# Linear attention block: x tile 1 transposed by the DMA crossbar instead of TensorE, and the Wk blocks dealt out anew over two DMA queues

## The chip, the cores and the metric

One core of one Trainium2 chip runs the kernel. The metric is device time in microseconds (us) of the whole program. The kernel before takes 99.58 us, the median of 3 runs (99.29 to 100.04).

## The reference: what is computed

```python
B, S, D = 1, 2048, 640;  H = 32; Dh = 20
qkv = (x @ wqkv)                       # split into q, k, v of 32 heads
phi = lambda t: where(t > 0, t + 1, exp(t)) + 1e-6
pq, pk = phi(q), phi(k)
kv  = einsum("bhsd,bhse->bhde", pk, v)
z   = einsum("bhsd->bhd", pk)
o   = einsum("bhqd,bhde->bhqe", pq, kv) / (einsum("bhqd,bhd->bhq", pq, z) + 1e-6)
return o @ wo
```

All inputs and the output are bfloat16. x is 2048 x 640, wqkv is 640 x 1920, wo is 640 x 640.

## The kernel before, in words

The 2048 rows of x are 16 tiles of 128 rows (st = 0 to 15); the 640 columns are 5 blocks of 128 (c = 0 to 4). Three of the buffers matter here. `xT` holds x transposed, which every projection needs as TensorE's stationary or moving operand. `xn` holds x as it lies in memory, which the later product of pk with x needs. `wk` holds the K columns of wqkv as five row blocks, called Wk blocks 0 to 4 (160 KB each).

The program is recorded by hand. `P.add(engine, ...)` appends an instruction to one engine's list and works out from the named tiles which semaphores it waits for. So the order on each engine is the order of the `P.add` calls. DMAs are instructions of the queue that issues them, SyncE ("sp") or ScalarE ("act").

TensorE's own order is: warm-up matmuls on constants (L283), the transposes of the first tiles (L200), the K projection of all 16 tiles (`k_half`, L293: two halves of 320 columns, five matmuls each, one for every block c), and after that the products of pk and x (L317), the Q projection (L354), the small products (L445, L472, L544) and the output projection (L576).

How the first stage is put together:

- `XCH` (L181) cuts the rows into seven pieces: tile 0, tile 1, tile 2, tiles 3 and 4, tiles 5 to 7, tiles 8 to 11, tiles 12 to 15. The first `NPE` = 2 pieces (L180) come through TensorE. The others come by `load_xT` (L187), one `dma_start_transpose` each on SyncE, straight from memory into `xT`.
- `load_wk` (L235) sets the order of the first DMAs. SyncE issues the left half of x tile 0, then Wk blocks 0, 2 and 3. ScalarE issues the right half of x tile 0, then x tile 1 ("x12"), then Wk blocks 1 and 4. In those strings "w23" is the block from 2 to 3.
- `load_xT` follows on SyncE with the five transposing DMAs, and `load_rest` (L258) with the Q weights, x tiles 2 to 15 for `xn` in three DMAs, the V weights and wo.
- `transpose_x(st, part)` (L193) transposes two or three 128 x 128 blocks of a tile on TensorE into PSUM; VectorE (part 0, L212) or ScalarE (part 1, L209) copies the result to `xT`.
- The string at L630 is TensorE's order for tiles 0 and 1: "k00a" is block 0 of tile 0, half a (one matmul), "t1a" is the first part of tile 1's transpose, "k10" is block 0 of tile 1, both halves (two matmuls). From tile 2 on each tile's ten matmuls stand together (L640).
- `k_phi` (L302) turns a tile's K into pk: an exponential on ScalarE, then two instructions on VectorE.

Of the kernel before, what the change touches and what calls it, by code (L numbers as in the profile page):

```python
# [84 lines left out]
def bass_standalone__linear_attn_block__prompt_kernel(nc, x, wqkv, wo, out):  # L85
# [15 lines left out]
    with contextlib.ExitStack() as ctx:  # L101
# [75 lines left out]
                    band(bm[:, GT * t:GT * (t + 1)], [[-DH if lo else DH, 3], [0, DH]],  # L177
                         -64 * t if lo else DH - 1 + 64 * t, 1 if lo else -1, "bm")

        NPE = 2  # L180
        XCH = [(0, 128), (128, 256),  # L181
               (256, 384), (384, 640), (640, 1024), (1024, 1536), (1536, 2048)]

        def xch_of(row):
            return next(i for i, (a, b) in enumerate(XCH) if a <= row < b)

        def load_xT():  # L187
            for i, (a, b) in enumerate(XCH[NPE:]):
                P.add("sp", lambda e, a=a, b=b: e.dma_start_transpose(
                    xT[:, :].rearrange("p (c s) -> p c s", s=S)[:, :, a:b], x[0, a:b, :]),  # L190
                    writes=[("xT", NPE + i)], dma=True)

# [22 lines left out]
        def xT_keys(a, b, cs=range(NC_)):  # L215
            keys = []
            for i, (p, q) in enumerate(XCH):
                if p < b and a < q:
                    keys += [("xT", i)] if i >= NPE else sorted(
                        {("xT", i, 0 if c < 2 else 2) for c in cs})  # L220
            return keys

        def w_cols(dst, lo, hi, col, key, eng):
            P.add(eng, lambda e: e.dma_start(
                dst[:, 0:NC_ * D].rearrange("p (c n) -> p c n", n=D)[:, :, lo:hi],
                wqkv[:, col + lo:col + hi].rearrange("(c p) n -> p c n", p=128)),
                writes=[key], dma=True)

        def load_xn(a, b, eng):
            P.add(eng, lambda e: e.dma_start(  # L230
                xn[:, a * D:b * D].rearrange("p (t n) -> p t n", n=D),
                x[0, 128 * a:128 * b, :].rearrange("(t p) n -> p t n", p=128)),
                writes=[("xn", t) for t in range(a, b)], dma=True)

        def load_wk():  # L235
            tl = mybir.InstLoadActFuncSet(
                name=nc.get_next_instruction_name(),
                act_func_set_id=ACT_TABLE_SET_LN_EXP, ins=[], outs=[])
            P.add("act", lambda e: e.add_instruction(tl), writes=["table"])
            for eng, lo in (("sp", 0), ("act", HALF)):  # L240
                P.add(eng, lambda e, lo=lo: e.dma_start(
                    xn[:, lo:lo + HALF], x[0, 0:128, lo:lo + HALF]),
                    writes=[("xn", 0, lo)], dma=True)
            for eng, what in (("sp", "w01 w23 w34"), ("act", "x12 w12 w45")):
                for k in what.split():
                    a, b = int(k[1]), int(k[2])
                    if k[0] == "x":
                        load_xn(a, b, eng)
                    else:
                        P.add(eng, lambda e, a=a, b=b: e.dma_start(  # L250
                            wk[:, a * D:b * D].rearrange("p (c n) -> p c n", n=D),
                            wqkv[128 * a:128 * b, D:2 * D].rearrange("(c p) n -> p c n", p=128)),
                            writes=[("wk", c) for c in range(a, b)], dma=True)
# [3 lines left out]

        def load_rest():  # L258
            w_cols(wqn, 0, D, 0, "wqn", "sp")
            for a, b in ((2, 8), (8, 12), (12, 16)):  # L260
                load_xn(a, b, "sp")
            for g, n in ((0, 5), (5, 1)):
                f = min(GT, gsz[g])
                k = gsz[g] // f * n
                for d in range(NC_):
                    P.add("sp", lambda e, g=g, f=f, k=k, d=d: e.dma_start(
                        wv[:, 128 * NG * d:128 * NG * (d + 1)].rearrange(
                            "p (j f) -> p j f", f=64)[:, 2 * g:2 * g + k, 0:f],
                        wqkv[128 * d:128 * (d + 1), 2 * D + goff[g]:2 * D + goff[g] + k * f].rearrange(
                            "p (j f) -> p j f", f=f)),  # L270
                        writes=[("wv", i, d) for i in range(g, g + n)], dma=True)
            for t in range(2):
                P.add("sp", lambda e, t=t: e.dma_start(
                    wog[64 * t:64 * t + GT, 0:5 * D].rearrange("p (g n) -> p g n", n=D),
                    wo[0:5 * GW, :].rearrange("(g t p) n -> t p g n", t=2, p=GT)[t]),
                    writes=[("wog", g, t) for g in range(5)], dma=True)
            P.add("sp", lambda e: e.dma_start(
                wog[0:gsz[5], 5 * D:6 * D], wo[goff[5]:, :]),
                writes=[("wog", 5, 0)], dma=True)

        def warm(n, cols=BK):
            for _ in range(n):
                P.add("pe", lambda e: e.matmul(  # L283
                    bank(4, cols), nc.const_aps.tensor(1.0, [128, 128], BF16),
                    nc.const_aps.tensor(1.0, [128, cols], BF16), start=True, stop=True),
                    writes=[("bank", 4)])
# [333 lines left out]

        pool_const()
        load_wk()
        load_xT()
        load_rest()
        warm(5)
        warm(1, 128)
        for part in range(2):
            transpose_x(0, part)
        warm(1)
        order = "k00a t1a k00b t1b k10 k01 k11 k02 k12 k03 k13 k04 k14"  # L630
        for k in order.split():
            st, part = int(k[1]), "ab".find(k[-1])
            if k[0] == "t":
# [127 lines left out]
```

## Time and profile before

| what | value |
|---|---|
| median of 3 runs | 99.58 us (99.29 to 100.04) |
| the profiled execution's own time | 99.56 us |
| its span in the profile | 98.3 us |
| TensorE matmuls (PE) busy | 95.1 us, 97% of the span |
| VectorE / ScalarE / GpSimd busy | 63.7 / 48.8 / 4.7 us |
| K projection, L293 | 160 matmuls, 22.8 us |
| DMA moved | 12.60 MB, mean 128 GB/s |

The span is what the profile covers, from the first to the last instruction; 1.26 us of the execution's time lie around it. In the profile PE is TensorE's matmul side and PEld its weight loads, DVE is VectorE, ACT is ScalarE, POOL is GpSimd, SP is SyncE. SPq and ACTq rows are DMA issues: their length is the time that the queue's sequencer spent on the issue, not the transfer. The landing of a transfer is given apart, counted from the start of its issue. A matmul's shown duration contains its pipeline, so the step from one start to the next is the rate. All times in microseconds are from the span's start, if nothing else is said.

### The profile page before, as it was taken

To read this page: it belongs to the slowest core of one execution; us is meant where nothing else is said; L and a number is where in the kernel's file an instruction comes from. 1 tells how busy PE (TensorE), PEld (TensorE's weight loads), DVE (VectorE), ACT (ScalarE), POOL (GpSimd) and SP (SyncE) were. 2 spreads that over 40 slices of the span, in tenths; PEclk is the share of its full clock that TensorE was granted. 3 is DMA by queue.
4 is the path that set the end of the run, shared out by engine and by line. 5 is a ranking of instruction groups with operands and counts; after the bars stand their busy time and mean duration, and the time that the engine had idled before them with its cause. 6 is when DMAs were issued, how large, how long until landed. Compare 5 with 4: busy or idle time off the path is not lost.

```text
span 98.3 us, 1814 instructions
## 1 busy us (share of the span) xinstructions
PE 95.1 (97%) x694; PEld 61.2 (62%) x699; DVE 63.7 (65%) x124; ACT 48.8 (50%) x93; POOL 4.7 (5%) x19
## 2 busy tenths in 40 slices
PE   6999999999999999999999999999999999999991
PEld 2467777777755444445687867655557677777771
DVE  5314998888899439997839836758999206272222
ACT  5116455544526120005806456796988765453532
POOL 6500000000000000000000520000000000000000
DMA  2999999999998294000340023313200335532334
GB/s 48 320 269 194 238 157 111 350 366 360 316 169 108 21 239 80 0 0 0 63 77 7 0 63 93 94 32 86 79 0 0 133 74 168 205 117 87 130 133 137
DMA packets 26369, 12.60 MB, mean 128 GB/s; under 512 B 18553, under 2 KB 26361, under 8 KB 26361
## 3 DMA queue, kind: packets, MB, share of 16 engines
q1 hardware_dynamic: 25640, 11.87, 50.2%
q10 hardware_dynamic: 720, 0.61, 1.9%
q8 instruction: 5, 0.08, 0.3%
q14 instruction: 4, 0.02, 0.1%
HBM read 5.90 MB, written 2.62 MB: 87 GB/s over the span
## 4 chain that ended last, share of the span: by engine, by line
PE 95%; ACT 2%; issue 0%
PE ps L293 23%; PE ps L576 22%; PE ps L354 22%; PE ps L317 21%; PE ps L283 3%; ACT w2g L483 2%; PE ps L445 1%; PE ps L544 1%; PE ps L200 1%; PE ps L472 1%; ACT osb L599 0%
## 5 line engine op out<-in xcount | busy, mean ns | idle before, releaser
L317 PE MATMUL ps<-pk,xn 128*128 128x480 bf16 (+1 forms) x160 | 23.2, 299 | 0.0
L293 PE MATMUL ps<-wk,xT 128*128 128x320 bf16 x160 | 22.8, 303 | 0.0
L354 PE MATMUL ps<-xT,wqn 128*128 128x512 bf16 x95 | 22.0, 379 | 0.4 <-issue 0.2
L576 PE MATMUL ps<-w2p,pq 128*128 128x320 bf16 (+2 forms) x170 | 22.1, 291 | 0.0
L293 PEld LDWEIGHTS ps<-wk,xT 128*128 128x128 bf16 x160 | 15.6, 98 | 6.8 <-DMA wk<-in_wqkv_dram 0.9
L576 PEld LDWEIGHTS ps<-w2p,pq 128*128 128x128 bf16 x170 | 15.9, 98 | 6.2 <-issue 0.2
L317 PEld LDWEIGHTS ps<-pk,xn 128*128 128x128 bf16 x160 | 13.6, 98 | 9.4 <-issue 0.3
L362 ACT ACTIVATE eq<-ps 128x512 bf16<-128x512 f32 x20 | 11.9, 597 | 13.8 <-PE ps L354 13.6
L354 PEld LDWEIGHTS ps<-xT,wqn 128*128 128x128 bf16 x100 | 11.5, 118 | 9.1 <-issue 0.3
L306 ACT ACTIVATE ek<-ps 128x640 bf16<-128x640 f32 x16 | 11.2, 704 | 10.7 <-PE ps L293 10.1
L599 ACT CAST osb<-ps 128x320 bf16<-128x320 f32 (+2 forms) x27 | 11.0, 413 | 9.7 <-PE ps L576 9.0
L311 DVE SCALAR_TENSOR_TENSOR pk<-ps,ek 128x640 bf16<-128x640 f32 x16 | 13.2, 825 | 0.5
L569 DVE TENSOR_TENSOR pq<-pq,rd 128x512 bf16<-128x512 bf16 x20 | 7.3, 418 | 4.2 <-DMA rd<-rdc 4.2
L375 DVE TENSOR_SCALAR eq<-eq 128x512 bf16<-128x512 bf16 x20 | 5.8, 288 | 5.9 <-ACT eq L362 5.8
L602 DVE CAST osb<-ps 128x320 bf16<-128x320 f32 (+1 forms) x7 | 3.2, 456 | 8.7 <-PE ps L576 8.7
L308 DVE TENSOR_SCALAR ek<-ek 128x640 bf16<-128x640 bf16 x16 | 5.2, 325 | 5.3 <-ACT ek L306 5.1
L366 ACT ACTIVATE rq<-ps 128x512 bf16<-128x512 f32 x13 | 7.7, 592 | 0.0
L339 ACT CAST pt<-ps 128x480 bf16<-128x480 f32 x4 | 2.2, 562 | 8.2 <-PE ps L317 8.1
L379 DVE TENSOR_TENSOR pq<-eq,rq 128x512 bf16<-128x512 bf16 x13 | 5.5, 426 | 1.1 <-ACT rq L366 0.7
L388 DVE TENSOR_TENSOR za<-pk 128x1280 f32<-128x1280 bf16 x4 | 5.8, 1482 | 0.0
L382 DVE SCALAR_TENSOR_TENSOR pq<-ps,eq 128x512 bf16<-128x512 f32 x7 | 4.8, 692 | 0.2
L388 DVE TENSOR_TENSOR za<-za 128x1280 f32<-128x1280 f32 x3 | 4.4, 1486 | 0.0
(37 smaller groups left out, 36.7 us busy)
## 6 DMA issues: line engine op xcount, KB each, us to landing
out_dram<-osb SPq DMA_DIRECT2D x15, 160.0 KB, 1.8
xn<-in_x_dram SPq DMA_DIRECT2D x2, 640.0 KB, 8.9
xn<-in_x_dram SPq DMA_DIRECT2D x1, 960.0 KB, 7.0
wqn<-in_wqkv_dram SPq DMA_DIRECT2D x1, 800.0 KB, 5.6
wv<-in_wqkv_dram SPq DMA_DIRECT2D x5, 150.0 KB, 5.1
wog<-in_wo_dram SPq DMA_DIRECT2D x2, 375.0 KB, 5.3
w2p<-w2g SPq DMA_DIRECT2D x10, 75.0 KB
rd<-rdc SPq DMA_DIRECT2D x8, 64.0 KB, 2.1
```

The costliest lines, as they stand in the source:

```text
L293: r = e.matmul(bank(b + h, HALF), xT[:, c * S + 128 * st:c * S + 128 * st + 128], wk[:, c * D + HALF * h:c * D + HALF * (h + 1)], start=(c ...
L306: P.add("act", lambda e: e.activation(fold(t[:, :]), two_banks(b), ACTF.Exp), reads=banks + ["table"], writes=[("ek", st % 3)])
L311: P.add("dve", lambda e: e.scalar_tensor_tensor(fold(pk[:, st * D:(st + 1) * D]), two_banks(b), 0.0, fold(t[:, :]), ALU.max, ALU.add), rea ...
L317: return e.matmul(bank(d // PB[h], PW[h], off=PW[h] * (d % PB[h])), xn[:, st * D + 128 * d:st * D + 128 * d + 128], pk[:, st * D + PO[h]:s ...
L354: r = e.matmul(bank(b), wqn[:, d * D:(d + 1) * D].rearrange("p (q c) -> p c q", c=NC_)[:, c, :], xT[:, d * S + BK * sbk:d * S + BK * (sbk ...
L362: P.add("act", lambda e: e.activation(t[:, :], bank(b), ACTF.Exp), reads=[("bank", b), "table"], writes=[("eq", i)])
L366: P.add("act", lambda e: e.activation(r[:, :], bank(b), ACTF.Relu), reads=[("bank", b), "table"], writes=[("rq", i)])
L375: P.add("dve", lambda e: e.tensor_scalar(t[:, :], t[:, :], 1.0, 1e-6, ALU.min, ALU.add), reads=[("eq", i)], writes=[("eq", i)])
L388: P.add("dve", lambda e: e.tensor_tensor(d_ap, a, b, ALU.add), reads=ra + rb, writes=[dst])
L569: P.add("dve", lambda e: e.tensor_tensor(v, v, rd[i][:, BK * h:BK * (h + 1)], ALU.mult), reads=[("rd", i, 2 * h), ("rd", i, 2 * h + 1), (" ...
L576: r = e.matmul(bank(b, hi - lo), pq[:, c * S + 128 * st:c * S + 128 * st + 128], w2p[:, c * D + lo:c * D + hi], start=(c == 0), stop=(c == ...
L599: P.add("act", lambda e: e.copy(osb[j][:, lo:hi], bank(b, hi - lo)), reads=[("bank", b)], writes=keys)
```

## The change

x tile 1 is no longer loaded ahead of the Wk blocks and transposed on TensorE. It becomes the first of six transposing DMAs, queued on SyncE between Wk blocks 0 and 4. ScalarE issues Wk blocks 1, 2 and 3. TensorE's string loses t1a and t1b, and the K matmuls of both tiles run in another order: blocks 0 to 2 of tile 0, blocks 0 to 2 of tile 1, then block 3 of both and block 4 of both. The natural copy of x tile 1 for `xn` now comes with tiles 2 to 7 in one later DMA.

```diff
-        NPE = 2
+        NPE = 1
...
-        def load_xT():
-            for i, (a, b) in enumerate(XCH[NPE:]):
+        def load_xT(*which):
+            for i in which:
+                a, b = XCH[NPE + i]
                 P.add("sp", lambda e, a=a, b=b: e.dma_start_transpose(
...
-            for eng, what in (("sp", "w01 w23 w34"), ("act", "x12 w12 w45")):
+            for eng, what in (("sp", "w01 t1 w45"), ("act", "w12 w23 w34")):
                 for k in what.split():
+                    if k[0] == "t":
+                        load_xT(0)
+                        continue
...
-            for a, b in ((2, 8), (8, 12), (12, 16)):
+            for a, b in ((1, 8), (8, 12), (12, 16)):
                 load_xn(a, b, "sp")
...
-        load_xT()
+        load_xT(*range(1, len(XCH) - NPE))
         load_rest()
...
-        order = "k00a t1a k00b t1b k10 k01 k11 k02 k12 k03 k13 k04 k14"
+        order = "k00 k01 k02 k10 k11 k12 k03 k13 k04 k14"
```

## Prediction

> **What bounds the kernel now.** I read the page's busy times and its chain first, to see which engine sets the end.
>
> ```profile
> PE 95.1 (97%) x694; PEld 61.2 (62%) x699; DVE 63.7 (65%) x124; ACT 48.8 (50%) x93; POOL 4.7 (5%) x19
> ...
> PE 95%; ACT 2%; issue 0%
> ```
>
> TensorE (PE) is busy for 97% of the span and is 95% of the chain that ended last. So a microsecond taken from TensorE's stream, or put into it, should reach the end nearly whole, wherever it lies. What matters is where the stream waits, and that is in the first 6 us. I read the timeline of the first 14 us for that.
>
> ```profile
> 0.79 0.40 SPq L241 DMA_DIRECT2D xn<-in_x_dram  x1
> ...
> 1.23 0.46 ACTq L230 DMA_DIRECT2D xn<-in_x_dram  x1
> 1.24 1.36 SPq L250 DMA_DIRECT2D wk<-in_wqkv_dram  x3
> ...
> 1.71 0.94 ACTq L250 DMA_DIRECT2D wk<-in_wqkv_dram  x2
> ...
> 2.65 12.30 SPq L189 DMA_TRANSPOSE xT<-in_x_dram  x5
> ...
> 4.19 0.10 PEld L293 LDWEIGHTS ps<-wk,xT 128*128 128x128 bf16 x1 [0.58 <-DMA wk<-in_wqkv_dram]
> 4.19 0.45 PE L293 MATMUL ps<-wk,xT 128*128 128x320 bf16 x1
> ...
> 5.24 8.95 PE L293 MATMUL ps<-wk,xT 128*128 128x320 bf16 x63
> ...
> 5.73 8.26 PEld L293 LDWEIGHTS ps<-wk,xT 128*128 128x128 bf16 x62 [0.34 <-DMA wk<-in_wqkv_dram]
> ```
>
> The reader is to see two waits: TensorE starts K at 4.19, when Wk block 0 lands, and its fifth K matmul waits for Wk block 1 until 5.73. From 5.73 on it runs without a gap. L317 starts at 26.93 in the timeline; tile 2's first matmul is the 17th after 5.73, so with s the step, 5.73 + 16 s + 140 s = 26.93 gives s = 0.136 us, and tile 2 starts at 7.91. Before 5.5 the steps are longer: the transposes start at 4.43 and the matmul before them at 4.19, and the two matmuls from 5.24 step by 0.26. The early matmuls thus run at about half rate, though the clock column of the view by windows shows 1.00 there.
>
> Then I asked for the transposing DMAs one by one, with their landings: tile 2; tiles 3 and 4; and, for an unloaded one of the same 128 x 640 size, the one of zh at 47.21.
>
> ```profile
> L189 SPq DMA_TRANSPOSE xT<-in_x_dram x1: 1329/1329/1329, 2.6 to 2.6; - x1
> ...
> DMA to landing us min/median/max: 4.6/4.6/4.6
> ```
> ```profile
> L189 SPq DMA_TRANSPOSE xT<-in_x_dram x1: 2130/2130/2130, 4.0 to 4.0; - x1
> ...
> DMA to landing us min/median/max: 5.0/5.0/5.0
> ```
> ```profile
> L423 SPq DMA_TRANSPOSE zt<-zh x1: 1348/1348/1348, 47.2 to 47.2; - x1
> ...
> DMA to landing us min/median/max: 2.7/2.7/2.7
> ```
>
> Tile 2 lands at 2.65 + 4.6 = 7.25 and is wanted at 7.91: 0.66 to spare. Tiles 3 and 4 are issued at 4.03, land at 9.03 and are wanted ten matmuls later, at 7.91 + 1.36 = 9.27: only 0.24 to spare. This is the tightest place of the whole K stage. The same query gives landings at 6.20 + 5.0 = 11.2 (tiles 5 to 7, wanted at 11.99), 7.85 + 6.7 = 14.55 (tile 8, wanted at 16.07) and 11.60 + 6.8 = 18.4 (tile 12, wanted at 21.5).
>
> **The change part by part.**
>
> *TensorE loses five transposes.* They step from 4.43 to 4.65 and from 4.92 to 5.24: 0.22 + 0.32 = 0.54 us of TensorE time. That is the most the removal can bring. Their copies (0.29 on VectorE, 0.48 on ScalarE) lie beside TensorE: both engines are next wanted for tile 0's exponential at 7.85. Nothing saved there.
>
> *ScalarE's queue* issues four DMAs before and after (the x half, then three blocks), done at 2.65, ahead of its first copy at 3.81. Nothing. Wk block 1 takes the place of x tile 1, issued at 1.23 and landed 3.1 later, at 4.3; K block 1 of tile 0 (4.19 + 2 x 0.26 = 4.7) then finds it there.
>
> *SyncE's queue.* Before, Wk blocks 2 and 3 stand between block 0 and tile 2's transpose: two issues of 0.43. After, it is tile 1's transpose and Wk block 4: 1.33 + 0.43. So tile 1's transpose is issued at 1.70, Wk block 4 at about 3.08, tile 2's at 3.55, and every later SyncE DMA 0.9 later than before.
>
> *When does tile 1 land (T1)?* From below: the unloaded price, 1.70 + 2.7 = 4.4. From above: tile 2's price in the full queue, 1.70 + 4.6 = 6.3. In between: Wk block 0, ahead of it in the queue, lands at 1.24 + 2.9 = 4.1; tile 2 landed 0.9 after the Wk block ahead of it (2.17 + 4.2 = 6.4, then 7.25); and it will share the DMA engines with blocks 2 and 3 on ScalarE's queue, 0.47 each at the 348 GB/s that the windows view shows from 3.75 to 5. That makes 4.1 + 0.9 = 5.0 without sharing and 5.9 with both. I take 5.7, because the full sharing is nearer to what tile 2 met.
>
> *What TensorE does with it.* Six matmuls of tile 0 run from 4.19, the first four or five at 0.26: done at about 5.6. Then it waits for T1, and 14 matmuls at 0.136 follow: tile 2 could start at T1 + 1.9 = 7.6. Before it started at 7.91. So 0.3 gained; the break-even is T1 = 6.0; at the bounds, T1 = 4.4 is no wait at all (20 matmuls, the first five at 0.26, from 4.19: 7.5, 0.4 gained) and T1 = 6.3 is 0.3 lost. [...]
>
> *When do tiles 3 and 4 land?* This decides. Before, they land 1.8 after tile 2 for two tiles' worth: 0.9 per tile. A transposed tile (0.9) now stands in the DMA engines ahead of them where a plain block (0.47) stood: 0.4 later, at 9.45. Bounds: 0 later if the engines have room (they moved only 110 GB/s from 8 to 9, just before that landing), and 0.9 later if all follows the issue: 9.03 to 9.95. A fortunate landing could even be earlier than before, since the 110 GB/s show that something other than the bytes held it; I allow 0.3 for that, the size of one tile's excess over the unhindered rate (0.9 against 160 KB at the 291 GB/s of 9 to 10, 0.56). I take 9.45, the work-conserving value, since tile 2's own start was set by the transfers ahead and not by its issue. Tile 3 then starts at 9.45 instead of 9.27: 0.2 lost, whatever tile 2 gained.
>
> [...]
>
> *Later DMAs* come 0.4 to 0.9 later, and that is covered: tiles 5 to 7 have 0.8 to spare plus the 0.2 lost, tile 8 has 1.5, tile 12 has 3.1. x tile 1 for `xn` adds 160 KB to a DMA that landed at 16.33 + 7.0 = 23.3; with 0.9 and 0.5 more it is 24.7, and L317 starts at 26.93. The Q weights (15.00 + 5.6 = 20.6) are wanted at 29.18. Were that cover gone, each would cost its lateness beyond the spare.
>
> *Sum.* 99.56 (the profiled execution; the median of the runs is 0.02 above) + 0.2 = 99.8 us.
>
> **The rivals.** A measurement of this kernel can tell about 1% (1.0 us) from no change.
>
> *A. Forecast: tiles 3 and 4 bind.* 99.8, own range 99.6 to 100.2.
>
> *B. The landings are covered, and the gain shows.* Tile 1 lands near 5.2 and tiles 3 and 4 no later than before. For it: 0.54 us of transposes gone and two waits of 0.9 together. Against it: the 0.24 to spare caps the gain there, unless that landing moves forward too; with the 0.3 allowed, the cap is 0.5. Time 99.1 to 99.5.
>
> *C. The later issue carries through whole.* Tiles 3 and 4 land 0.9 later or a little more: 0.9 - 0.24 = 0.7 lost; tile 1 at its own upper bound would cost 0.3, which lies within that. For it: SyncE needs 1.33 to 3.70 for each transpose's issue, back to back. Against it: tile 2's transpose waited behind other transfers, not for its issue. Time 100.2 to 100.6.
>
> *D. Slower: TensorE's early half rate lasts.* The rate changes between 5.24 and 5.73, after warm-up matmuls made for nothing else. If the wait for tile 1 (5.6 to 5.7, or to 6.3) puts that off, the 14 matmuls up to tile 2 cost 0.26 - 0.136 = 0.125 more each: 1.75 lost, 101.3. It decides from eight matmuls on (1.0 us). For it: a new idle stretch just there. Against it: before, TensorE idled for 0.23 in the same place and the rate rose all the same, and the real matmuls now stand closer from 4.19 on.
>
> **How the numbers follow.** A 0.47, B 0.28, C 0.18, D 0.07. Predicted is A, 99.8. The range leaves out D and the upper end of C, and below B's end: 99.1 to 100.8, since C's bounds reach beyond 100.6 if tiles 5 to 7 also lose their cover by 0.2. Slower by over 1% (100.6): D's 0.07 and 0.06 of C, 0.13. Faster by over 1% (98.6): no row gives 1.0 us, as 0.54 is the most that leaves TensorE; 0.02. Within 1%: 0.85.
>
> **What would show it.** T1: the landing of the transpose issued at 1.70, and the idle time before tile 1's first L293 row. The cap: an idle stretch of TensorE before tile 3 with the transposing DMA as its end, and the landing of the two-tile transpose at 9.3 to 9.6. D: steps of 0.26 after 6 us. The forecast is wrong if tile 1 lands after 6.5, if tiles 3 and 4 land before 9.1 or after 10, or if another gap of over 0.3 appears in TensorE's stream after 12 us.

## The result and the profile after

The changed kernel is slower: the ratio to the kernel before is 1.0117, 95% interval 1.0078 to 1.0156, about 1.2 us on 99.9. Forecast were 99.8 us and 99.1 to 100.8. The ratio goes by the five of its eleven executions that took 100.35 to 101.62 us; the other six took 102.2 to 104.05, and with them its median is 102.2 us. In four of the six TensorE's granted clock falls for 3.4 us. One profile was taken with such a fall (span 101.1 us, 102.34 us) and one without (span 99.4 us, 100.64 us). The second is read first.

TensorE's weight loads in the timeline, second profile of the changed kernel (start, length, what, and in brackets the idle time before it and what ended it):

```profile
4.52 0.75 PEld L297 LDWEIGHTS ps<-wk,xT 128*128 128x128 bf16 x6 [0.93 <-DMA wk<-in_wqkv_dram]
7.07 5.00 PEld L297 LDWEIGHTS ps<-wk,xT 128*128 128x128 bf16 x38 [1.80 <-DMA xT<-in_x_dram]
```

Here is the whole loss. The six matmuls of tile 0 run from 4.52, 0.3 later than planned, and then TensorE stands for 1.5 us (the matmul row beside it has 1.47) until tile 1's transpose lands. From 7.08 it runs without a gap: 14 matmuls of 0.136 put tile 2's start at 8.98, against 7.91 before. That is 1.07 later, and the span is 1.1 longer (99.4 against 98.3). The two transposing DMAs on which the forecast stood, from the view of the tile xT; first tile 1's:

```profile
L190 SPq DMA_TRANSPOSE xT<-in_x_dram x1: 1331/1331/1331, 1.7 to 1.7; - x1
...
DMA to landing us min/median/max: 5.3/5.3/5.3
```

then that of tiles 3 and 4:

```profile
L190 SPq DMA_TRANSPOSE xT<-in_x_dram x1: 1952/1952/1952, 5.0 to 5.0; - x1
...
DMA to landing us min/median/max: 4.9/4.9/4.9
```

Tile 1 lands at 1.70 + 5.3 = 7.0, where 5.7 was forecast and 6.3 was the upper bound. Tiles 3 and 4 land at 4.96 + 4.9 = 9.8, inside the forecast's 9.03 to 9.95, but nobody waits for them any more: tile 3 could not start before 8.98 + 1.36 = 10.34. The view by windows shows what the DMA engines did meanwhile (last column GB/s), first the kernel before:

```profile
3.50:4.50 1.00, 1.00 (x6) 0.34 (x5) 0.28 (x1) 0.48 (x1) 0.39 (x2) 1.00 0.96 333
4.50:5.50 1.00, 1.00 (x8) 0.71 (x7) 0.29 (x1) 0.02 (x1) 0.00 (x0) 1.00 1.07 368
```

and then the changed kernel's second profile:

```profile
3.50:4.50 1.00, 0.68 (x4) 0.09 (x1) 0.26 (x1) 0.48 (x1) 0.39 (x2) 1.00 1.08 334
4.50:5.50 1.00, 0.97 (x6) 0.47 (x6) 0.00 (x0) 0.00 (x0) 0.00 (x0) 1.00 1.30 197
5.50:6.50 1.00, 0.11 (x1) 0.00 (x0) 0.00 (x0) 0.00 (x0) 0.00 (x0) 1.00 1.03 222
```

Until 4.5 both move the same. Then the kernel before, which serves plain blocks from both queues, moves 368 GB/s, and the changed kernel, with tile 1's transpose on one queue and Wk block 3 on the other, 197. The engines are busy all the time (share 1.30), so it is the transfers that are slow, not the supply. The low rate alone does not say that the two queues are the cause: in the runs below in which tile 1 is early, the same stretch has 180 to 232 GB/s (194 where only transposes are in flight).

The first profile, with the clock's fall. Its weight loads and the view by windows (the third column from the right is the granted clock):

```profile
7.14 4.89 PEld L297 LDWEIGHTS ps<-wk,xT 128*128 128x128 bf16 x25 [1.60 <-DMA xT<-in_x_dram]
```
```profile
7.00:8.00 1.00, 0.86 (x4) 0.52 (x5) 0.00 (x0) 0.00 (x0) 0.00 (x0) 0.57 1.16 256
8.00:9.00 1.00, 1.00 (x6) 0.54 (x5) 0.00 (x0) 0.00 (x0) 0.00 (x0) 0.50 0.97 216
9.00:10.00 1.00, 1.00 (x5) 0.59 (x4) 0.00 (x0) 0.00 (x0) 0.00 (x0) 0.50 1.14 159
10.00:11.00 1.00, 1.00 (x7) 0.61 (x6) 0.00 (x0) 0.44 (x1) 0.00 (x0) 0.72 1.27 285
```

Tile 1 lands at the same place, but from 7.14 on the clock is halved: 0.86 + 1 + 1 + 0.56 = 3.4 us of it, the matmul steps in the trace are 0.267, and tile 2 starts at 10.71, 2.8 late. The span is 2.8 longer (101.1 against 98.3).

### The profile page after: what moved, and what is told of

Its sections match the earlier page's. It is cut to its first block, busy times and chain, and to the rows that moved or that the text cites. A ratio compares the mean times of both kernels' runs of the same rounds, so it can differ in the third digit from the quotient of the medians.

```text
span 101.1 us, 1807 instructions
## 1 busy us (share of the span) xinstructions
PE 96.4 (95%) x694; PEld 61.0 (60%) x694; DVE 63.4 (63%) x123; ACT 48.2 (48%) x92; POOL 4.7 (5%) x19
## 4 chain that ended last, share of the span: by engine, by line
PE 91%; DMA 5%; SPq 1%; issue 0%; ACT 0%
PE ps L297 23%; PE ps L580 22%; PE ps L321 22%; PE ps L358 21%; DMA xT<-in_x_dram 5%; PE ps L449 1%; PE ps L548 1%; PE ps L476 1%; SPq L254 0%; SPq L242 0%; ACT osb L603 0%
## 5 line engine op out<-in xcount | busy, mean ns | idle before, releaser
L297 PE MATMUL ps<-wk,xT 128*128 128x320 bf16 x160 | 24.0, 313 | 1.9 <-DMA xT<-in_x_dram 1.3
L358 PE MATMUL ps<-xT,wqn 128*128 128x512 bf16 x100 | 23.1, 379 | 0.0
L437 POOL TENSOR_SCALAR zb<-hm,zc 128x32 bf16<-128x32 bf16 x5 | 1.9, 412 | 54.0 <-DVE zc L432 54.0
```

The costliest lines, as they stand in the source:

```text
L297: r = e.matmul(bank(b + h, HALF), xT[:, c * S + 128 * st:c * S + 128 * st + 128], wk[:, c * D + HALF * h:c * D + HALF * (h + 1)], start=(c ...
L358: r = e.matmul(bank(b), wqn[:, d * D:(d + 1) * D].rearrange("p (q c) -> p c q", c=NC_)[:, c, :], xT[:, d * S + BK * sbk:d * S + BK * (sbk ...
```

## Experiments

The theory after the result, M: a transposing DMA and plain copies in the other queue hold each other up in the DMA engines, far beyond their bytes. Rivals: F, the first transposing DMA from memory is slow by itself; Q, a copy behind it in its own queue is as bad. For the clock, C: the idle stretch causes the fall. The diffs show of each changed line only the part that changes, and "..." stands for lines left out.

**Nothing beside tile 1's transpose** (e1_behind)

```diff
-(("sp", "w01 t1 w45"), ("act", "w12 w23 w34"))
+(("sp", "w01 t1 w23 w34 w45"), ("act", "w12"))
```

> The changed kernel with Wk blocks 2 and 3 moved from ScalarE's queue to SyncE's, behind tile 1's transpose and ahead of block 4; ScalarE issues only block 1. Nothing but the tail of block 1 is now in the other queue while tile 1's transpose is served. Theory M (a transposing DMA and plain copies of the other queue hold each other up in the DMA engines): tile 1, which landed at 7.1 in the changed kernel's profile, lands at 5.0 to 5.6, TensorE's idle stretch before tile 1 falls from 1.4 us to under 0.3 or moves to block 2, and tile 2 starts before 9. Rival F (the first transposing DMA from memory is slow by itself): tile 1 still lands at 6.5 to 7.1. Rival Q (behind it in its own queue is as bad as beside it): 6.5 or later too, which the run with the copies beside and the lone run tell from F.

```profile
L190 SPq DMA_TRANSPOSE xT<-in_x_dram x1: 1327/1327/1327, 1.7 to 1.7; - x1
...
DMA to landing us min/median/max: 3.6/3.6/3.6
```

Tile 1 landed at 1.70 + 3.6 = 5.3. F and Q are out: the same instruction, issued at the same moment, with three blocks behind it, lands 1.7 earlier. The kernel was no faster (1.0136, interval 1.0083 to 1.0189), since block 2 now stood behind the transpose, and TensorE waited for it until 6.79:

```profile
6.79 4.24 PEld L297 LDWEIGHTS ps<-wk,xT 128*128 128x128 bf16 x20 [1.90 <-DMA wk<-in_wqkv_dram]
```

At full clock the 16 matmuls left would have put tile 2 at 6.80 + 16 x 0.136 = 8.98. "Before 9" failed because in this profile the clock fell as well: tile 2 started at 10.66. Serving the blocks behind the transpose did not let more be moved in all: from 3.5 to 7.0 the view by windows has 239 GB/s here and 246 in the changed kernel's second profile.

**All copies beside, none behind** (e2_beside)

```diff
-(("sp", "w01 t1 w45"), ("act", "w12 w23 w34"))
+(("sp", "w01 t1"), ("act", "w12 w23 w34 w45"))
```

> The changed kernel with Wk block 4 moved from SyncE's queue, where it stood behind tile 1's transpose, to the end of ScalarE's. All plain copies are now beside the transposes and none behind. Theory M: tile 1 lands at 6.8 to 7.5, no better than in the changed kernel, and block 4 lands late as well. Rival Q (the block behind it in its own queue held it up): tile 1 lands before 6.2.

```profile
L190 SPq DMA_TRANSPOSE xT<-in_x_dram x1: 1335/1335/1335, 1.7 to 1.7; - x1
...
DMA to landing us min/median/max: 5.5/5.5/5.5
```

7.2, as M says; Q is out a second time. The ratio, 1.0276 (1.0225 to 1.0326), holds more than this landing: in its profile TensorE's steps were 0.267 from tile 1's landing up to 10.1. They had been about as long for the six matmuls before the wait (4.32, 4.56, 4.82, 5.09), and the granted clock's column has 1.00 throughout. So here the half rate of the start lasted, as rival D of the forecast has it, rather than coming back.

**Nothing but the tail of block 1 beside, and the other blocks held back** (e4_lone). Blocks 2, 3 and 4 wait for the landing.

```diff
-(("sp", "w01 t1 w45"), ("act", "w12 w23 w34"))
+(("sp", "w01 t1"), ("act", "w12 w23 w34 w45"))
...
-P.add(eng, lambda e, a=a, b=b: e.dma_start(
+P.add(eng, after=[P.writers[("xT", 1)]] if a > 1 else [], fn=lambda e, a=a, b=b: e.dma_start(
```

> The changed kernel with Wk blocks 2, 3 and 4 issued by ScalarE only after tile 1 has landed (a wait on its semaphore). Tile 1's transpose has only other transposes behind it, and nothing beside it but the tail of block 1. The time gets worse, since the blocks come late; the number wanted is tile 1's landing. Theory M: 4.9 to 5.4. Rival F (slow by itself): 6.5 or later.

```profile
L190 SPq DMA_TRANSPOSE xT<-in_x_dram x1: 1327/1327/1327, 1.7 to 1.7; - x1
...
DMA to landing us min/median/max: 3.8/3.8/3.8
```

5.5, just past the expected 4.9 to 5.4 and far from F's 6.5. The held-back blocks then met the later transposes, and took, from issue at 5.49, 5.85 and 6.54 to landing, 4.5, 6.9 and 8.4 us in the trace; in the kernel before a Wk block takes 2.9 to 4.5. The whole took 109.16 us. So copies are late beside transposes, too.

**One block beside** (e6_one_beside)

```diff
-(("sp", "w01 t1 w45"), ("act", "w12 w23 w34"))
+(("sp", "w01 t1 w34 w45"), ("act", "w12 w23"))
```

> The changed kernel with Wk block 3 alone moved from ScalarE's queue to SyncE's behind tile 1's transpose: one block (2) beside the transpose, two (3 and 4) behind. Theory M, by dose: tile 1 lands between the run with nothing beside it (5.3) and the changed kernel (7.1), at 5.7 to 6.5. Rival (only the bytes count, 0.47 a block): 5.8 here, but then 6.3 with two beside, where 7.1 was measured.

Tile 1's transpose, and TensorE's weight loads:

```profile
L190 SPq DMA_TRANSPOSE xT<-in_x_dram x1: 1314/1314/1314, 1.7 to 1.7; - x1
...
DMA to landing us min/median/max: 3.8/3.8/3.8
```
```profile
5.54 0.66 PEld L297 LDWEIGHTS ps<-wk,xT 128*128 128x128 bf16 x6 [0.51 <-DMA xT<-in_x_dram]
6.46 0.93 PEld L297 LDWEIGHTS ps<-wk,xT 128*128 128x128 bf16 x8 [0.26 <-DMA wk<-in_wqkv_dram]
8.26 1.20 PEld L297 LDWEIGHTS ps<-wk,xT 128*128 128x128 bf16 x10 [0.87 <-DMA xT<-in_x_dram]
10.26 0.79 PEld L297 LDWEIGHTS ps<-wk,xT 128*128 128x128 bf16 x7 [0.80 <-DMA xT<-in_x_dram]
```

5.5: one block beside costs 0.2 or less, the second one (block 3) 1.5. It is not a dose that grows evenly, and 5.5 is earlier than the expected 5.7. The packets in the trace show what differs. Tile 1 is 640 packets of 256 bytes, the first at 3.98 and half of them started by 4.51; block 2's last packet on ScalarE's queue starts at 4.40. In the changed kernel block 3's packets start from 4.51 to 6.14. Tile 1's last packet starts at 5.01 here and the tile lands 0.5 later; in the changed kernel's second profile it starts at 5.86 and the tile lands 1.2 later. So of the 1.5 us some 0.85 go by before the last packet starts, and 0.7 between that and the landing.

All ten times lie between 100.2 and 100.77, none with the clock's fall; the ratio is 1.0052 (1.0026 to 1.0079). The last two rows are what is left with tile 1 early: TensorE waits for tile 2 until 8.26, and then, until 10.26, for tiles 3 and 4, the forecast's own step, which sets the end 1.0 late in this profile (span 99.3).

**A block of x in block 3's place** (e8_x_beside), from the kernel of the last run

```diff
-(("sp", "w01 t1 w34 w45"), ("act", "w12 w23"))
+(("sp", "w01 t1 w34 w45"), ("act", "w12 w23 x12"))
...
-for a, b in ((1, 8), (8, 12), (12, 16)):
+for a, b in ((2, 8), (8, 12), (12, 16)):
```

> The run with one block beside tile 1's transpose (Wk block 3 behind it on SyncE; tile 1 landed at 5.5), with a second block put back beside it on ScalarE's queue, but of x instead of wqkv: the 160 KB of x tile 1 for xn, whose rows lie one after the other in memory, taken out of a late DMA. Theory M2 (a block that is still unserved in the other queue when the transpose is half read slows both, whatever it holds): tile 1 lands at 6.6 to 7.3, as with Wk block 3 there. Rival S (it is the strided rows of wqkv): tile 1 lands at 5.4 to 6.0.

```profile
L190 SPq DMA_TRANSPOSE xT<-in_x_dram x1: 1332/1332/1332, 1.7 to 1.7; - x1
...
DMA to landing us min/median/max: 5.1/5.1/5.1
```

6.8. TensorE doesn't need this block at all, and still tile 1 comes 1.3 later than without it. What the block holds, and whether its rows are strided, is not the cause; that a block comes while the transpose is under way is (M2 in the text above): none of its 128 packets had started when tile 1 was half read, at 4.54. Two of the four times have the clock's fall (102.37 and 102.78); the others are 100.52 and 100.71.

**The same in the kernel before** (e7_before_beside and e9_before_two_beside): x tile 2, or tiles 2 and 3, on ScalarE behind Wk block 4, beside tile 2's transpose.

```diff
-("act", "x12 w12 w45")
+("act", "x12 w12 w45 x23")
...
-for a, b in ((2, 8), (8, 12), (12, 16)):
+for a, b in ((3, 8), (8, 12), (12, 16)):
```

The second one has x24 and (4, 8).

> The kernel before, with the 160 KB of x tile 2 for xn taken out of a late DMA of SyncE and issued by ScalarE right after Wk block 4, so that one more plain block lies beside tile 2's transpose; nothing else changes, and TensorE's order is that of the kernel before. Theory M: tile 2's transpose, which landed at 7.2, lands at 8.1 or later, past the 7.91 at which TensorE wants it, tiles 3 and 4 land after 9.6, and the time grows by 0.3 to 1.5 us. Rival (only the bytes count): tile 2 lands at 7.7, tiles 3 and 4 at 9.5, the time grows by 0.2 at most.

> The kernel before, with x tiles 2 and 3 for xn (320 KB in one DMA) issued by ScalarE right after Wk block 4 instead of late by SyncE: two blocks beside tile 2's transpose instead of the one of the earlier run, where tile 2 landed at 7.8 and the time did not change clearly. Theory M2: tile 2 now lands at 8.7 or later, TensorE waits for it at 7.9, and the time grows by 0.7 or more. Rival B (only the bytes count, 0.47 a block): tile 2 lands at 8.2 to 8.3, tiles 3 and 4 no later than 9.9, the time grows by 0.3 to 0.6.

Tile 2's transpose with one block more, and with two:

```profile
L189 SPq DMA_TRANSPOSE xT<-in_x_dram x1: 1327/1327/1327, 2.6 to 2.6; - x1
...
DMA to landing us min/median/max: 5.2/5.2/5.2
```
```profile
L189 SPq DMA_TRANSPOSE xT<-in_x_dram x1: 1329/1329/1329, 2.6 to 2.6; - x1
...
DMA to landing us min/median/max: 6.0/6.0/6.0
```

With one, 7.8, and no clear change of time (1.0017, 0.9985 to 1.0049): there the count of bytes was right, and M as first stated was wrong. With two, 8.7 against the bytes' 8.2 to 8.3: past 7.91, TensorE waited, and the time grew (1.0054, 1.0031 to 1.0076, about 0.5 us, less than the 0.7 expected). So M needs a condition. M2's fits the runs on tile 1 and the run with one block here: a block costs no more than about its bytes if it is served by the time the transpose is half read (all of block 2 above; 123 of 128 packets of x tile 2 here, though only 19 came before the transpose's first), and much more if it is still to come (1.3 and 1.5 for the two that were). With two blocks the tile lands where M2 put it, but not for M2's reason: 252 of their 256 packets had started when tile 2 was half read, at 7.50. The time is what rival B said (0.3 to 0.6). So this pair doesn't show the condition; it stands on the runs on tile 1.

**TensorE kept at work while it waits** (e3_fill): six warm-up matmuls before block 0 of tile 1.

```diff
-order = "k00 k01 k02 k10 k11 k12 k03 k13 k04 k14"
+order = "k00 k01 k02 f6 k10 k11 k12 k03 k13 k04 k14"
...
+            elif k[0] == "f":
+                warm(st)
```

> The changed kernel with six warm-up matmuls of 512 columns on constants (six times 0.216 us, on the bank that tile 2 will write) put between block 2 of tile 0 and block 0 of tile 1, so that TensorE works while it waits for tile 1. They feed nothing into the result. Theory C (TensorE's half rate after the wait comes from the idle stretch): no steps of 0.267 after 7 us, the granted clock stays 1.00 in all slices, the time is 100.3 to 100.8 in all runs, and none lies at 102 or above as most do for the changed kernel. Rival (the half rate has another cause, or a cause of the chip): steps of 0.267 return after 7 us, and times of 102 remain.

```profile
5.50 1.11 PEld L287 LDWEIGHTS ps<-const-bfloat16-1.0 128*128 128x128 bf16 x6
6.97 4.05 PEld L297 LDWEIGHTS ps<-wk,xT 128*128 128x128 bf16 x31 [0.37 <-DMA xT<-in_x_dram]
```

Tile 1 lands about as late as in the changed kernel (6.9), and the steps after 6.97 are 0.136. All eight times lie from 100.44 to 101.27, where six of the changed kernel's eleven were 102.2 or more (four of the six with a mean granted clock of 0.983, which is half the rate for 3.4 of 101 us). The ratio is 1.009 (1.0055 to 1.0125). Three of the eight are above the expected 100.8. C holds for the changed kernel: with TensorE at work in the gap no execution has the fall, where 4 of its 12 had, and what is left, 0.9 to 1.0 us, goes with tile 1's landing. The gap isn't the only cause: the kernel before, without such a gap, has the same mean clock of 0.983 in 2 of the 50 executions listed beside these runs (102.58 and 102.56 us).

**All blocks ahead of the transpose** (e5_blocks_first; e5_again is the same kernel)

```diff
-(("sp", "w01 t1 w45"), ("act", "w12 w23 w34"))
+(("sp", "w01 w23 w45 t1"), ("act", "w12 w34"))
...
-order = "k00 k01 k02 k10 k11 k12 k03 k13 k04 k14"
+order = "k00 k01 k02 k03 k04 k10 k11 k12 k13 k14"
```

> The changed kernel with every Wk block ahead of tile 1's transpose: SyncE issues blocks 0, 2, 4 and then the transpose, ScalarE issues blocks 1 and 3, and TensorE runs all five blocks of tile 0 before those of tile 1. No copy stands behind the transpose or, but for the tail of block 4, beside it. Theory M (copies and transposes hold each other up): tile 1 lands at 6.0 to 6.8, TensorE waits for it less than 0.8 us, tile 2 starts at 7.6 to 8.2, the granted clock stays 1.00, time 99.6 to 100.3, about that of the kernel before. Rival A (the forecast: what binds is the landing of tiles 3 and 4, and here their transposes are issued 1.4 later than before): TensorE idles before tile 3 instead, with that transpose landing at 9.9 to 10.4, and the time is 100.4 to 100.9. Rival F (the first transposing DMA from memory is slow by itself): tile 1 lands at 7.5 or later.

> The kernel with all blocks ahead of tile 1's transpose once more, for a profile at TensorE's full clock: it took 1.005 of the time before. Theory: TensorE waits for tile 1 (landing near 6.5) by 0.3 to 0.6 and again before tile 3 (landing near 10.0), which sets the end, 0.5 to 0.9 later than before. Rival: the wait for tile 1 alone makes the 0.5.

One of the first run's twelve executions, the profiled one, took 562 us, with TensorE slow throughout; the other eleven times are 100.03 to 100.88, ratio 1.0048 (1.0024 to 1.0073). The second run's weight loads:

```profile
6.85 2.56 PEld L297 LDWEIGHTS ps<-wk,xT 128*128 128x128 bf16 x20 [0.55 <-DMA xT<-in_x_dram]
10.19 0.79 PEld L297 LDWEIGHTS ps<-wk,xT 128*128 128x128 bf16 x7 [0.78 <-DMA xT<-in_x_dram]
```

Tile 1 lands at 2.65 + 4.2 = 6.8 and hardly matters. TensorE waits before tile 3 until 10.19, which is 0.9 later than before, and the span is 99.2, 0.9 longer. Here rival A, the forecast's own mechanism, sets the end. None of these kernels beats the kernel before.

The changed kernel's second profile was read above (after_again):

> The changed kernel once more, for a second profile. In all theories tile 1 lands at 6.6 to 7.2. If TensorE's clock does not fall after the wait, tile 2 starts 1.9 after that landing, at 8.6 to 9.1, and the time is 100.3 to 101.0; if it falls, 102 or more.

## Why the prediction was wrong

- *TensorE's stream sets the end, and a delay before tile 2 reaches it whole.* Right: 1.07 at tile 2's start, 1.1 in the span; with the clock's fall 2.8 and 2.8.
- *Five transposes less save 0.54 and the copies nothing.* Right, but worthless: TensorE was done with its six matmuls at 5.45 and then waited.
- *ScalarE's queue costs nothing; Wk block 1 comes at 4.3.* About right: 4.3 in the first profile, 4.7 in the second.
- *When does tile 1 land: 5.7, within 4.4 to 6.3.* This step failed: 7.0 to 7.1. The base was sound (5.3 with nothing beside, where the working had 5.0). The sharing was mis-sized: 0.47 for each of blocks 2 and 3, by bytes at 348 GB/s. Measured: at most 0.2 for block 2 and 1.5 for block 3, the one that was still to come when the transpose was half read. The upper bound was no bound, since tile 2's 4.6 came from a place where the other queue was nearly served (in the trace of before ScalarE's queue had 36 of its 576 packets left at 5.5, and tile 2's transpose was half read at 5.84). The forecast's own sign of being wrong, tile 1 after 6.5, came true. The slow rows in the trace of before gave no warning of this: from 8 to 9, at 110 GB/s, only transposes were in flight (every packet is under 512 bytes, a plain block's has 1280).

```profile
DMA packets 430, 0.11 MB, mean 110 GB/s; under 512 B 430, under 2 KB 430, under 8 KB 430
```

- *Tile 2 can start at T1 + 1.9.* The 1.9 held at full clock (7.08 to 8.98). But the working left out when tile 2 itself lands: at 3.70 + 4.3 = 8.0 in the changed kernel, and at 4.14 + 4.1 = 8.2 in the run with one block beside (issued 0.4 later there), where tile 1 had come at 5.5 and TensorE waited for tile 2. So the 0.3 to be gained from T1 = 5.7 was not to be had.
- *What landed beside tile 1.* Block 3, on ScalarE's queue, landed with tile 1 at 7.1 in the first profile (2.20 + 4.9); block 2, ahead of it there, landed at 5.4 (1.71 + 3.7). From the start of tile 1's last packet to its landing it takes 1.2 us with two blocks beside and 0.5 with one; no run shows what fills the 0.7 more. Packets of both queues were in flight together: from 5.0 to 5.5 in the first profile 36 of ScalarE's queue and 73 of SyncE's. Whether a transpose and a copy so mixed cost more in all than one after the other is not shown: the last of tile 1 and the Wk blocks lands at 3.08 + 4.2 = 7.3 in the changed kernel, at 4.2 + 3.4 = 7.6 with blocks 2 to 4 behind the transpose, and at 3.7 + 3.1 = 6.8 with one beside.
- *Tiles 3 and 4 decide, at 9.45.* The mechanism is real and the landing, 9.8, lies in its bounds, but it decided nothing in the changed kernel, where tile 1's delay covers it. It decides in the two variants in which tile 1 does not hold TensorE up (10.26 and 10.19), where it comes later than the bounds.
- *Rival D, the half rate, 0.07.* It happens in part of the executions, at the price given: 13 steps of about 0.267 instead of 0.136, 1.7 us. The argument against it, an earlier idle stretch of 0.23 without harm, did not carry over to one of 1.5. Two forms are seen: a rate that had been full falls back after the wait (the first profile), and the half rate of the start lasts (the run with all copies beside).
- *The range.* That the ratio gives 100.7, just inside 100.8, is luck: that end was there for late landings behind tile 2, not for tile 1.

What stays open: why a copy and a transpose that alternate are so slow. The trace shows it (in both profiles, packets of 1280 bytes of ScalarE's queue, most of which take 55 ns before 4.5, took 148 to 201 ns on average in the half microseconds from 5 to 6), but no run looked inside a DMA engine. Open too is what fills the 0.7 of the 1.5 us that go by after tile 1's last packet has started.

## What to carry to other kernels

A transfer that a wait depends on should not be priced by the bytes alone of what shares the DMA engines with it when one of the two is a transposing DMA: here 0.47 a block by bytes, and at most 0.2 and then 1.5 measured. The GB/s of a stretch with both kinds in flight is nearer and still too kind: the kernel before has one (5.5 to 6.5, 223 GB/s), and 0.73 for each of the two blocks would have put tile 1 at 6.5, where 7.0 was measured. A run that moves one block and reads the landing is surer. Keep the other queue empty while a transpose that is waited for is served (tile 1 landed at 5.3 so, at 7.0 with two blocks beside), and price the landings of the transposes behind it as well: here they set the end when tile 1 no longer did (TensorE waited for tile 3 until 10.26 and 10.19), and no variant beat the kernel before. A late landing can cost TensorE more than the wait: with the clock's fall after it, tile 2 started 2.8 late, without it 1.07. With six matmuls on constants in the gap none of eight executions had the fall.

## What the runs showed of the hardware

- Tile 1's landing with plain blocks 2 to 4 placed differently: none beside 5.3 (or 5.5 with no copy behind either), one 5.5, two 6.9 to 7.1, three 7.2; two with the second of x instead of wqkv 6.8.
- In the first profile TensorE's granted clock fell to 0.50 for 3.4 us after the wait for tile 1 (1.27 us before its matmuls, 1.60 before their weight loads). It did not fall in the second profile, after a wait of 1.47 and 1.80. The profiles do not show what decides; in the eight executions with work in the gap it did not fall.
- The granted clock's column shows such a fall (0.50), but not the half rate at the start: it has 1.00 while steps are 0.26, in the run with all copies beside up to 10.1 us. Two of the changed kernel's six long executions (104.05 and 102.37 us) also have a mean granted clock of 1.00, and no profile shows why they were long. The steps of the matmuls are the surer sign.
